# A conditioned block of linear attention and a spatial gate on one core: its projections as 64-row pairs over two token tiles

## The chip, the cores and the metric

The kernel runs on 1 core of one Trainium2 chip. The metric is device microseconds of one execution, the median of the runs shown, lower is better. TensorE is called PE below, its weight loads PEld, VectorE DVE, ScalarE ACT, GpSimd POOL and SyncE SP; SP and ACT issue the transfers.

## The reference, cut to what matters

2048 tokens of width 448 pass through two sub-blocks, each behind a normalisation whose scale and shift come from a condition vector `c`. The first sub-block is linear attention with 16 heads of 28; the second is a gated unit of half-width 896 whose gate mixes tokens with a 2048 by 2048 matrix.

```
mod = (silu(c) @ w_mod).reshape(1, 6, 1, 448)          # sa, ca, ga, sb, cb, gb
h = layernorm(x) * (1 + ca) + sa
q, k, v = split(h @ wqkv)                              # 16 heads of 28
pq, pk = q @ w_phi, k @ w_phi                          # per head
phi_q = [softmax(pq), softmax(-pq)]; phi_k likewise    # 56 features a head
kv, z = phi_k^T v, sum over tokens of phi_k
o = (phi_q kv) / (phi_q z + 1e-6)
x = x + ga * (o @ wo)
h = layernorm(x) * (1 + cb) + sb
z1, z2 = halves of gelu(h @ w_in)                      # 896 each
g = w_sp @ layernorm(z2) + b_sp
out = x + gb * ((z1 * g) @ w_out)
```

## The kernel before, in words

Tokens lie in 16 tiles of 128 (tile `i`). The width 448 is the contraction of every projection, and it lies on partitions as four blocks of 112 (`CB`, `KC` = 4), so a projection of one tile is a chain of four matmuls with 112 rows in use. A 113th row of the first block holds ones: the shift of the norm is multiplied into the weights (`SH`, `SHw`, the tile `Ga` or `Gb`), and the scale is multiplied onto the weights' rows (`SC`, `SCw`). `YB` does the shift for the half of `w_in` that is used transposed.

Everything on the main path is written as short steps, and one string, `ORDER`, lists them in the order in which they are issued: `kM:3@5` is the step `kM` for tile 3 into PSUM slot 5, a suffix `/V`, `/S`, `/G` or `/Y` picks DVE, ACT, POOL or the SP queue. Slots `A0`, `A1`, `A2` and `C` are pairs of PSUM banks, a digit is one bank. Each engine works through its own steps in the order of the string.

The steps that the text speaks of, with their lines before:

- start: `ld` loads, `l1s` statistics of a tile of `x` (L845, L846), `l1e`, `l1r`, `l1a` the normalised tile in the buffer `xpad` (L849 to L856), `X` a transpose on PE (L869) or `T1` one by a transfer (L861), both into `hT`; `ct`, `ce` the condition vector; `cs`, `cc` the columns of scale and shift (L767); `FT`, `ET`, `PF`, `EP` fold `w_phi` into the weights of k and q (L822, L828, L838).
- first stage: `kM`, `vM`, `qM` the projections (L879, L887, L927), `kE` and `kF` the two exponentials of k (L882), `qE` and `qF` those of q (L932), `vC` a copy of v, `kS`, `kR`, `kP` the softmax of k (L893, L897, L900), `kA` the sum over tokens of features times values (L910), `KV` its masked copy.
- second stage: `nM` the numerators and the two sums of a tile (L955), then on ACT `nX` and on DVE `nC`, `nS`, `nV`, `nT` (L959 to L974): a weight per head and the weighted numerators; `nA` adds the two softmax halves (L980); `T2` transposes the result, `wM` multiplies by `wo` (L990), `wR` adds it to `x` (L997), `wQ` sums its squares (L1002), `lA` to `lD`, `l2r`, `l2a` normalise again (L1010 to L1025) into `xpad`, and `T3` transposes that into `hT` over the first norm's.
- third stage: `zM` and `zG` the half that is normalised (L1036, L1040), `zQ` to `zN` its norm; `yM` and `yG` the other half (L1066, L1069), four tiles at a time.
- last stage: the gate's token product, `gM` and `pM` (L1082, L1146, the latter by seven products for eight blocks, with sums `tT` and `sS` ahead), its additions, and `oM`, `oH` the output (L1095, L1100).

Each of the last stage's matmuls uses all 128 rows. A flag, set from the largest softmax sum, chooses at the end whether a general version runs as well; it does not run here.

## Time and profile before

| what | us |
|---|---|
| median of 2 runs (248.64 to 248.87) | 248.75 |
| the profiled execution's span, first to last instruction | 246.4 |
| the profiled execution's own time | not given apart from its span |
| first k matmul | 13.67 |
| first numerators | 54.52 |
| first `zM` matmul | 74.98 |
| first matmul of the last stage on the chain | 134.15 |
| last matmul done | 241.94 |

The span leaves out what lies ahead of the first instruction and behind the last, 2.35 us between the median and the span. In the views a row names line, engine, operation, what it writes and reads, and shapes as partitions times elements. The duration of a matmul is that from its start to its modelled end; matmuls follow each other more closely than that, and the pitch is read from the chain that ended last, where a row gives the start, the time and the count of a run of matmuls.

### The profile page before, as it was taken

To read this page: it belongs to the slowest core of one execution; us is meant where nothing else is said; L and a number is where in the kernel's file an instruction comes from. 1 tells how busy PE (TensorE), PEld (TensorE's weight loads), DVE (VectorE), ACT (ScalarE), POOL (GpSimd) and SP (SyncE) were. 2 spreads that over 40 slices of the span, in tenths; PEclk is the share of its full clock that TensorE was granted. 3 is DMA by queue.
4 is the path that set the end of the run, shared out by engine and by line. 5 is a ranking of instruction groups with operands and counts; after the bars stand their busy time and mean duration, and the time that the engine had idled before them with its cause. 6 is when DMAs were issued, how large, how long until landed. Compare 5 with 4: busy or idle time off the path is not lost.

```text
span 246.4 us, 4186 instructions
## 1 busy us (share of the span) xinstructions
PE 238.6 (97%) x1505; PEld 126.3 (51%) x1513; DVE 184.2 (75%) x371; ACT 115.5 (47%) x232; POOL 125.1 (51%) x174
## 2 busy tenths in 40 slices
PE   7999999999899999999999999999999999999992
PEld 5854566665455555454444444444444544444652
DVE  3899989877998988666568983659989667386552
ACT  2899888749999797888997111000020000000000
POOL 4759986755877976965521059209239400052000
PEclk9999999999999999999999999999999999999999
DMA  7994999950226976543420870009900111000022
GB/s 188 292 284 98 213 272 201 233 141 21 64 67 150 169 133 128 129 88 85 95 33 4 170 130 0 0 3 167 197 19 3 37 56 56 3 0 3 19 71 75
DMA packets 68800, 25.23 MB, mean 102 GB/s; under 512 B 58401, under 2 KB 68642, under 8 KB 68770
## 3 DMA queue, kind: packets, MB, share of 16 engines
q1 hardware_dynamic: 68016, 24.35, 47.0%
q10 hardware_dynamic: 754, 0.52, 0.7%
q8 instruction: 14, 0.23, 0.4%
q14 instruction: 16, 0.13, 0.2%
HBM read 8.87 MB, written 1.84 MB: 43 GB/s over the span
## 4 chain that ended last, share of the span: by engine, by line
PE 92%; DVE 1%; ACT 1%; issue 1%; POOL 1%; DMA 1%; DVEq 0%; POOLq 0%
PE f_psum L1146 29%; PE f_psum L1066 10%; PE f_psum L1036 9%; PE f_psum L1095 8%; PE f_psum L927 6%; PE f_psum L1082 6%; PE f_psum L879 5%; PE f_psum L887 5%; PE f_psum L990 4%; PE f_psum L910 3%; PE f_psum L955 3%; DMA f_x<-in_A_x_dram 1%; PE f_psum L781 1%; ACT f_Eq L932 1%; PE f_psum L786 1%
## 5 line engine op out<-in xcount | busy, mean ns | idle before, releaser
L1146 PEld LDWEIGHTS <-f_z2n 128*128 128x128 bf16 x192 | 18.7, 98 | 22.4
L1146 PE MATMUL f_psum<-f_wsp,f_z2n 128*128 128x512 bf16 x119 | 27.2, 379 | 0.1
L1198 POOL TENSOR_TENSOR f_z1T<-f_gb,f_z1T 128x512 bf16<-128x512 f32 x6 | 8.4, 1411 | 35.8 <-DVE f_gb L1173 35.8
L1036 PE MATMUL f_psum<-f_win,f_hT 112*128 112x448 bf16 (+1 forms) x128 | 26.1, 352 | 0.0
L1066 PE MATMUL f_psum<-f_hT,f_win 112*128 112x512 bf16 x112 | 26.0, 379 | 0.0
L1146 PE MATMUL f_psum<-f_hT,f_Eq 128*128 128x512 bf16 x92 | 22.3, 379 | 0.2
L1166 ACT COPY f_Eq<-f_psum 128x512 f32<-128x512 f32 x4 | 2.3, 585 | 38.6 <-PE f_psum L1146 38.6
L1095 PE MATMUL f_psum<-f_wout,f_z1T 128*128 128x448 bf16 x105 | 20.4, 352 | 0.0
L1069 ACT ACTIVATE f_z1T<-f_psum,f_yb 128x512 bf16<-128x512 f32 x28 | 18.0, 682 | 1.8 <-PE f_psum L1066 1.8
L1036 PEld LDWEIGHTS <-f_hT 112*128 112x128 bf16 (+1 forms) x128 | 12.3, 97 | 11.7
L932 ACT ACTIVATE f_Eq<-f_psum 112x1024 bf16<-112x1024 f32 x16 | 15.9, 1028 | 4.3 <-PE f_psum L927 4.2
L893 DVE TENSOR_REDUCE f_ksum<-f_E 128x32 f32<-128x896 bf16 x16 | 16.8, 1064 | 1.3 <-ACT f_E L882 1.3
L882 ACT ACTIVATE f_E<-f_psum 128x448 bf16<-128x448 f32 x32 | 16.2, 565 | 2.7 <-PE f_psum L879 2.7
L974 DVE TENSOR_TENSOR f_t<-f_psum,f_w 128x896 bf16<-128x896 f32 x16 | 16.9, 1086 | 0.5
L1066 PEld LDWEIGHTS <-f_win 112*128 112x128 bf16 x112 | 10.8, 98 | 12.3
L1040 ACT ACTIVATE f_z2g<-f_psum 128x896 bf16<-128x896 f32 x16 | 14.6, 914 | 4.8 <-PE f_psum L1036 4.0
L900 POOL TENSOR_TENSOR f_phik<-f_E,f_kr 128x896 bf16<-128x896 bf16 x8 | 14.1, 1765 | 4.4 <-DVE f_kr L897 3.6
L1111 DVE TENSOR_TENSOR f_xpad<-f_psum,f_x 128x448 bf16<-128x448 f32 x15 | 9.2, 621 | 8.5 <-PE f_psum L1095 8.3
L1146 PEld LDWEIGHTS <-f_Eq 128*128 128x128 bf16 x96 | 9.4, 98 | 11.3
L1095 PEld LDWEIGHTS <-f_z1T 128*128 128x128 bf16 x105 | 10.2, 98 | 9.4
L927 PE MATMUL f_psum<-f_hT,f_Wq 113*128 113x512 bf16 (+1 forms) x64 | 15.0, 378 | 0.0
L887 PE MATMUL f_psum<-f_wv,f_hT 113*128 113x448 bf16 (+1 forms) x64 | 14.5, 352 | 0.0
(213 smaller groups left out, 498.1 us busy)
## 6 DMA issues: line engine op xcount, KB each, us to landing
out_dram<-f_xpad SPq DMA_DIRECT2D x15, 112.0 KB, 1.8
...
```

The lines of the kernel that those rows point to most:

```text
L882: nc.scalar.activation(out=Er[i % NR][:, s, :], in_=ps["k" + str(i)][:, 0, 0:D], func=ACT.Exp, scale=1.0 - 2.0 * s)
L887: nc.tensor.matmul(t[:, 0, 0:D], lhsT=hT[0:KR[m], i, m, :], rhs=wv[0:KR[m], m, :], start=(m == 0), stop=(m == KC - 1))
L893: nc.vector.tensor_reduce(out=ksum[:, i], in_=Er[i % NR][:].rearrange("p s (c f h) -> p (s c) h f", c=4, h=HP), axis=AX.X, op=ALU.add)
L927: nc.tensor.matmul(t[:, u, :], lhsT=Wq[0:KR[m], m, cc * CB:cc * CB + P], rhs=hT[0:KR[m], 4 * st:4 * st + 4, m, :], start=(m == 0), stop=(m ...
L932: nc.scalar.activation(out=Eq[st // 2][0:CB, 2 * c2:2 * c2 + 2, s, (st % 2) * 512:(st % 2 + 1) * 512], in_=ps["q" + str(n)][0:CB, :, :], f ...
L974: nc.vector.tensor_tensor(out=tr[i % 2][:], in0=numv(i)[:, :, :, 0:DH], in1=wr[i // 2 % 2][:, i % 2].unsqueeze(3).to_broadcast([P, 2, H, D ...
L1036: nc.tensor.matmul(t[:, hf, 0:D], lhsT=hT[0:KR[m], i, m, :], rhs=win_s[0:KR[m], m, FH + hf * D:FH + (hf + 1) * D], start=(m == 0), stop=(m ...
L1066: nc.tensor.matmul(t[:, 0, :], lhsT=win_s[0:CB, m, fc * P:(fc + 1) * P], rhs=hT[0:CB, 4 * st:4 * st + 4, m, :], start=(m == 0), stop=(m == ...
L1069: nc.scalar.activation(out=stage_b()["z1T"][:, fc, st * 512:(st + 1) * 512], in_=ps["y%d_%d" % (st, fc)][:, 0, :], func=ACT.Gelu_apprx_tan ...
L1082: nc.tensor.matmul(g[:, 0, 0:b - a], lhsT=later["z2n"][:, s_, fc * P:(fc + 1) * P], rhs=wspT[t][:, s_, a:b], start=(s_ == 0), stop=(s_ == ...
L1095: nc.tensor.matmul(ps["o" + str(t)][:, 0, 0:D], lhsT=later["z1T"][:, fc, t * P:(t + 1) * P], rhs=wout_s[:, fc, :], start=(fc == 0), stop=( ...
L1146: nc.tensor.matmul(t[:, 0, :], lhsT=b[:, j, f * P:(f + 1) * P], rhs=a[:, j, :], start=(PSTART[k] and j == 0), stop=(j == NH - 1), skip_gro ...
```

## The change: the width in seven blocks of 64, two token tiles on the two halves of the partitions

The width is cut into 7 blocks of 64 (`NB`, `HB`). A pair `p` of token tiles stands together: block `j` of tile 2p on partitions 0 to 63, of tile 2p+1 on partitions 64 to 127 (`HALF`). The weights are loaded twice, once for each half (`load_half`). A projection of a pair is 7 times 2 matmuls of 64 rows that alternate between the halves and write to two PSUM banks (`pairs_mm`, and the same loop in `qM`, `wM`, `zM` and `yM`). `kM`, `vM`, `wM` and `zM` now take pairs (8 of each), `yM` takes four pairs at once (14 instead of 28), and `qM` has 256 columns a matmul instead of 512.

```diff
-    def kM(i, slot):
-        t = ps["k" + str(i)] = bank(slot, "k_ps")
-        for m in range(KC):
-            nc.tensor.matmul(t[:, 0, 0:D], lhsT=hT[0:KR[m], i, m, :], rhs=Wk[0:KR[m], m, :], start=(m == 0), stop=(m == KC - 1))
+    def pairs_mm(t, p, w, n):
+        for j in range(NB):
+            for h in range(2):
+                nc.tensor.matmul(t[:, h, 0:n], lhsT=hT[HALF[h], p, j, :], rhs=w[HALF[h], j, 0:n], start=(j == 0), stop=(j == NB - 1))
+    def kM(p, slot):
+        t = ps["k" + str(p)] = bank(slot, "k_ps")
+        pairs_mm(t, p, Wk, D)
```

Scale and shift leave the weights: `SH`, `SC`, `SHw`, `SCw`, `YB`, `YE` and the row of ones are gone. `cf` and `ec` make scale and shift as columns on partitions, and `md` applies them to the transposed tiles in `hT`, in place, 128 partitions by 256 columns a step, 21 such steps for the first norm and 28 for the second; for the first two pairs the copy `XE` behind the PE transpose does it in 14 steps of 128 columns.

```diff
+    def cf(u, slot):
+        t = ps["cf%d" % u] = bank(slot, "cf_ps")
+        o = (u % 2) * D
+        for j in range(NB):
+            for kk in range(KC):
+                for h in range(2):
+                    nc.tensor.matmul(t[HALF[h], 0, j:j + 1], lhsT=wm1[:, kk, o + j * HB:o + (j + 1) * HB], rhs=scol[:, kk:kk + 1],
+                                     start=(kk == 0), stop=(kk == KC - 1))
+    def modulate(eng, out_, in_, u, j):
+        sh, sc = mods[u][:, 0, j:j + 1], mods[u][:, 1, j:j + 1]
+        if eng is nc.scalar:
+            nc.scalar.activation(out=out_, in_=in_, func=ACT.Identity, scale=sc, bias=sh)
+        else:
+            eng.tensor_scalar(out=out_, in0=in_, scalar1=sc, scalar2=sh, op0=ALU.mult, op1=ALU.add)
+    def md(u, a, b, j0, j1, eng):
+        for j in range(j0, j1):
+            v = hT[:, a:b, j, :]
+            modulate(eng, v, v, u, j)
```

`PF` is written in two column halves, 64 columns of weights each, 112 matmuls for k and q instead of 32. The sums and the numerators are pairs too: `kA` adds in two banks, one for each half of the tokens' rows, and `kb`, `kc`, `km` join them; `nM` takes four heads' 56 features on each half.

```diff
-        for s in range(2):
-            for cc in range(4):
-                o0 = s * D + cc * CB
-                nc.tensor.matmul(ps["kv"][:, s, cc * 116:(cc + 1) * 116], lhsT=pr[i % NR][:, o0:o0 + P],
-                                 rhs=vr[i % NR][:, cc * HP:(cc + 1) * HP, :].rearrange("p h f -> p (h f)"),
+        for t in range(2):
+            for a in range(8):
+                for h in range(2):
+                    nc.tensor.matmul(ps["kv"][:, h, a * 58:(a + 1) * 58], lhsT=PRT[HALF[h], p % NF, t, 2 * a:2 * a + 2, :].rearrange("p a e -> p (a e)"),
+                                     rhs=VRT[HALF[h], p % NR, t, 2 * a:2 * a + 2, :].rearrange("p h f -> p (h f)"),
-                nc.tensor.matmul(t[:, s, cc * 120:(cc + 1) * 120], lhsT=E[0:CB, cc, s, o:o + P],
-                                 rhs=KVbd[0:CB, s, cc, :, :].rearrange("p h d -> p (h d)"), start=True, stop=True)
+                for h in range(2):
+                    r = slice(HB * h, HB * h + U)
+                    nc.tensor.matmul(t[:, h, (s * 4 + cc) * 60:(s * 4 + cc + 1) * 60], lhsT=E[r, cc, s, o:o + P],
+                                     rhs=KVbd[r, s, cc, :, :].rearrange("p h d -> p (h d)"), start=True, stop=True)
```

Steps that read PSUM follow in width: `kE` 16 times 896 columns instead of 32 times 448, `vC` 8 times 896, `yG` 14 times 1024 instead of 28 times 512, `kS` 8 times 1792 columns. `wR` is always on DVE. Rings are shorter: `xpad` holds 4 pairs (8 tiles, as before), features of k 2 pairs instead of 4 tiles, the half behind `zG` 4 tiles instead of 5, outputs 5 tiles instead of 8. `cA` for the first block adds a sum that `pb` has made instead of the bias.

`ORDER` is new from end to end. Its part around the numerators, before and after:

```diff
-kA:15@A0 wos:2/V ge:1 qM:3@C qE:3 KV:1 KV:0 nM:0@A1 ... nM:1@A2 ... YB@0 ... SHw:2@1 ... qM:4@C ... SHw:3@2 ... nM:3@A2 ... nM:2@A0 ... qM:5@A1 ... zM:1@A2
+kA:7@A2 cf:3@2 kb qE:6,1 kc qM:5@A0 km:0,1 km:0,0 km:1,1 km:1,0 ... nM:0@A2 nM:1@C nX:0 nM:2@A1 ... nM:3@A0 ... nM:4@C ... nM:5@A2 ... nM:6@A0 ... nM:7@A1
+... wM:0@A2 ... nM:8@C ... nM:9@A2 ... wM:1@A1 ... wM:2@A0 ... nM:10@A1 ... nM:11@A0 ... wM:3@C ... nM:12@A2 ... nM:13@A1 ... zM:0@A0@C ... wM:4@A2 wM:5@A1
```

Before, four of the eight `qM` are issued ahead of the first `nM` and four behind it, and the first `zM` comes when ten `nM` are issued; after, all eight `qM` are ahead of the first `nM`, and the first `zM` comes behind `nM:13`. The first `zM` after needs the slots `A0` and `C`, which `nT:11` and `wR:7` leave, and both pairs of `md:1,0,2`.

On DVE the work around the first numerators stood so before (`f_cr` is written by `nC`, `f_dn` by `nS`, `f_w` by `nV`, `f_t` by `nT`, `f_win` is part of the weights that `SCw` scales):

```order
L962 TENSOR_TENSOR f_cr_101<-f_psum,f_Sx 128x32 x2
L966 TENSOR_TENSOR f_dn_103<-f_cr_101 128x32
L967 RECIPROCAL f_dn_103<-f_dn_103 128x32
L795 COPY f_yb<-f_psum 128x7
L971 TENSOR_TENSOR f_w_105<-f_Sx,f_dn_103 128x64
L974 TENSOR_TENSOR f_t<-f_psum,f_w_105 128x896 x2
L801 TENSOR_SCALAR f_win<-f_psum,f_cb_80 113x448
L944 TENSOR_TENSOR f_wout<-f_wout,f_g_rep 128x448
```

And after, where the additions to `x` (`f_x`, `wR`) of the second group begin (rows of the fourth and fifth pair of tiles):

```order
L989 SCALAR_TENSOR_TENSOR f_x,f_s_86<-f_psum,f_x 128x448 x2
L967 TENSOR_TENSOR f_w_104<-f_Sx,f_dn_102 128x64
L970 TENSOR_TENSOR f_t<-f_psum,f_w_104 128x2x2x224
L976 TENSOR_TENSOR f_oo<-f_t 128x7x64
L957 TENSOR_TENSOR f_cr_99<-f_psum,f_Sx 128x32 x2
L970 TENSOR_TENSOR f_t<-f_psum,f_w_104 128x2x2x224
L989 SCALAR_TENSOR_TENSOR f_x,f_s_86<-f_psum,f_x 128x448 x2
L961 TENSOR_TENSOR f_dn_101<-f_cr_99 128x32
L962 RECIPROCAL f_dn_101<-f_dn_101 128x32
```

The steps for a pair of tiles are the same as before; the scaling of weights between them is gone, and the additions to `x` of tiles 0 to 7 stand between the numerators, ahead of the first `zM`.

On ACT, this stood before the first two `zG` (`f_z2g`) before:

```order
L1002 ACTIVATE f_junk,f_s_88<-f_x 128x448 x2
L932 ACTIVATE f_Eq<-f_psum 112x2x512 x2
L799 ACTIVATE f_win<-f_win,f_cb_80 112x896
L959 COPY f_Sx<-f_psum 128x32 x2
L738 ACT_TABLE_LOAD
L738 ACTIVATE f_warm<-f_warm 128x1
L1040 ACTIVATE f_z2g,f_zs_91<-f_psum 128x896 x2
```

And this stands there after (`f_hx` holds `hT`, `f_mod` the columns of scale and shift):

```order
L993 ACTIVATE f_junk,f_s_87<-f_x 128x448 x4
L954 COPY f_Sx<-f_psum 128x32 x2
L782 ACTIVATE f_hx<-f_hx,f_mod_81 128x2x128 x5
L954 COPY f_Sx<-f_psum 128x32
L782 ACTIVATE f_hx<-f_hx,f_mod_81 128x2x128
L954 COPY f_Sx<-f_psum 128x32
L993 ACTIVATE f_junk,f_s_87<-f_x 128x448 x2
L1044 ACTIVATE f_z2g,f_zs_90<-f_psum 128x896 x2
```

The exponentials of q and the table load have moved ahead, and six of the seven `md` steps of the first two pairs stand directly ahead of the first `zM` and its `zG` (the seventh is on POOL).

On the SP queue the loads at the start were, before (`f_wm` are the columns of the condition's matrix for shift and scale):

```order
L664 DMA f_x<-in_A_x_dram 128x448
L653 DMA f_wq_raw<-in_A_wqkv_dram 112x4x448
L665 DMA f_x<-in_A_x_dram 128x448
L657 DMA f_phi<-in_A_w_phi_dram 112x4x28
L660 DMA f_wm_120<-in_w_mod_dram 112x4x464 x2
```

And after:

```order
L669 DMA f_x<-in_A_x_dram 128x2x448
L669 DMA f_x<-in_A_x_dram 128x448
L663 DMA f_phi<-in_A_w_phi_dram 112x4x28
L669 DMA f_x<-in_A_x_dram 128x448
L669 DMA f_x<-in_A_x_dram 128x4x448
L656 DMA f_qa<-in_A_wqkv_dram 112x4x448
L669 DMA f_x<-in_A_x_dram 128x4x448
L666 DMA f_wm_118<-in_w_mod_dram 112x4x448 x2
```

Two groups of four tiles of `x` now stand ahead of the condition's columns.

582 lines of the change are left out of this document (274 added, 308 removed).

## The prediction

> **What bounds the kernel now.** I read the page first, then who waited for whom on PE, then the chain that ended last, then the stretches between the chain's landmarks.
>
> The page's span and first part, and two rows of the waits of PE (engine and line, what it waited for, us in total, times, longest):
>
> ```profile
> span 246.4 us, 4186 instructions
> PE 238.6 (97%) x1505; PEld 126.3 (51%) x1513; DVE 184.2 (75%) x371; ACT 115.5 (47%) x232; POOL 125.1 (51%) x174
> ...
> PE f_psum L955 <- DVE f_t L974: 1.1, 2, 0.7
> PE f_psum L988 <- ACT f_Eq L932: 0.4, 1, 0.4
> ```
>
> PE is busy 97% of the time and waits 1.5 us for other engines' results after its start. So the kernel is its stream of matmuls, and less matmul time is a gain as long as nothing else takes PE's place. The chain (start, us, work, count) gives the pitches and the landmarks:
>
> ```profile
> 9.94 0.38 PE f_psum L767 x16
> ...
> 13.67 1.52 PE f_psum L879 x8
> ...
> 29.00 1.74 PE f_psum L927 x8
> ...
> 36.61 0.42 PE f_psum L910 x8
> ...
> 52.76 1.74 PE f_psum L927 x8
> 54.52 1.01 PE f_psum L955 x16
> 55.53 0.68 PE f_psum L792 x28
> 56.21 0.78 PE f_psum L786 x4
> ...
> 74.98 3.04 PE f_psum L1036 x16
> ...
> 126.38 7.77 PE f_psum L1066 x36
> 134.15 0.22 PE f_psum L1082
> ...
> 241.96 0.39 DVE f_xpad L1104
> ```
>
> A matmul of 448 columns costs 1.52/8 = 0.19 us, one of 512 columns 0.217, one of 116 columns 0.052, and one of a single column with its weight load 0.38/16 = 0.024. The last stage runs from 134.15 to 241.94 without a gap worth naming, and 4.46 us lie behind the last matmul. The stretches show how near the other engines stand to PE (busy us of PE, PEld, DVE, ACT, POOL):
>
> ```profile
> 13.67:54.52 40.85, 40.83 (x337) 24.03 (x335) 37.41 (x77) 31.76 (x62) 32.18 (x37) 1.00 0.96 206
> 54.52:74.98 20.46, 19.43 (x176) 11.69 (x177) 17.80 (x45) 18.82 (x37) 14.15 (x16) 1.00 0.23 52
> 74.98:134.15 59.17, 58.77 (x329) 29.75 (x328) 43.27 (x117) 50.24 (x108) 36.76 (x70) 1.00 0.55 103
> ```
>
> Up to 75 us DVE is busy nine tenths of the time. The stretch to look at is the second: from the first numerators to the first `zM` PE is full, and DVE at 17.80 and ACT at 18.82 of 20.46 us nearly are. PE is full there because four `qM` (6.9 us), two `SHw` (1.5) and `YB` (0.7) are put between the numerators.
>
> **The change part by part: PE's work.** No row shows two matmuls at work at once. If the two halves of a pair overlap wholly, a pair costs one stream of columns; if not at all, two, since a matmul's time goes by columns and not by the rows in use:
>
> ```profile
> L879 PE MATMUL f_psum<-f_Wk,f_hT 112*128 112x448 bf16 x48 | 11.7, 351 | 0.0
> L1095 PE MATMUL f_psum<-f_wout,f_z1T 128*128 128x448 bf16 x105 | 20.4, 352 | 0.0
> ```
>
> I take one stream, which is the assumption on which the change stands, and keep the other end as a rival. Then k, v, `wM` and `zM` are 56+56+56+112 = 280 pairs at 0.19 = 53.2 us, `yM` 98 at 0.217 = 21.3, `qM` 112 of 256 columns at half of 0.217 = 12.2: 86.7 us. Before they are 320 matmuls at 0.19 and 176 at 0.217: 99.0. That is 12.3 off, and `SH`, `SHw` (20 at 0.19) and `YB` take 4.5 more away. On: `cf` has 224 single-column matmuls for 64, 160 at 0.024 = 3.8 (half of that if its column halves overlap). `kA` and `nM` have 256 matmuls each of half the columns instead of 128: between 0.024 and half of 0.052 each, so 6.1 to 6.7 us against 6.7, nil. `PF` has 112 for 32, beside loads that PE awaits at the start anyway. Sum: 13 us less matmul work. That alone would give 246.4 - 13 = 233.
>
> **Where the 13 us go.** The new order must be followed through its landmarks. First k matmul: it needs `XE`, three steps of which stand on DVE behind ten `l1s` and the small steps of the weights.
>
> ```profile
> L845 DVE BATCH_NORM_STATS2 f_st<-f_x 128x6 f32<-128x448 bf16 x16 | 9.7, 604 | 1.1 <-DMA f_x<-in_A_x_dram 1.1
> L846 DVE BATCH_NORM_AGGREGATE f_mv<-f_st 128x2 f32<-128x6 f32 x16 | 2.9, 182 | 0.5
> L828 DVE CAST f_Wk<-f_psum 112x448 bf16<-112x448 f32 x1 | 0.6, 614 | 0.0
> L759 DVE TENSOR_TENSOR f_BD<-f_phi,f_bmask 112x448 bf16<-112x448 bf16 x1 | 0.6, 612 | 0.0
> 3.44 0.64 DVE f_st L845
> ```
>
> Ten times 0.76 (busy over count, both rows) is 7.6; three evictions at 0.62 and 0.8 for the block-diagonal in two halves are 2.7, seven steps on a few columns some 1.2: 11.5 us from about 3.5, when the first `x` is there, to 15.0, then 0.8 for `XE`. So the first k matmul starts at about 15.8 instead of 13.67. Two groups of `x` also stand ahead of the condition's columns in the SP queue now, and `cf` is no earlier for that.
>
> From there to the first numerators the order holds on PE: `kM` and `vM` 21.3, `qM` 12.2, `kA` 6.2, two `gr` 1.5, two `cf` 2.7: 43.9 us. DVE, ACT and POOL get about what they had there (less for `SC`, fewer and wider exponentials, plus 21 `md` of 0.26 to 0.55 us): 32 to 38 us each, beside PE. But k, v and q now fill pairs of banks, three of which are left once the sums hold the fourth, and the third k pair waits for `md` steps behind `kP` on POOL; I put 2.5 us for that, between 0 and 6. First numerators: 15.8 + 43.9 + 2.5 = 62.2.
>
> Then the stretch that decides. All `qM` are done, `SHw` and `YB` are gone, so until the first `zM` PE has 14 `nM` at 0.39 and four `wM` at 1.33: 10.8 us. `zM:0` waits for `nT:11` and `wR:7` on DVE. One pair of tiles costs DVE, in the timeline of before (start, us, engine, line):
>
> ```profile
> 55.66 0.31 DVE L962 TENSOR_TENSOR f_cr<-f_psum,f_Sx 128x32 f32<-128x32 f32 x2 [0.91 <-ACT f_Sx L959]
> 56.01 0.19 DVE L966 TENSOR_TENSOR f_dn<-f_cr 128x32 f32<-128x32 f32 x1
> 56.24 0.35 DVE L967 RECIPROCAL f_dn<-f_dn 128x32 f32<-128x32 f32 x1
> 56.62 0.23 DVE L971 TENSOR_TENSOR f_w<-f_Sx,f_dn 128x64 f32<-128x64 f32 x1
> 56.88 2.09 DVE L974 TENSOR_TENSOR f_t<-f_psum,f_w 128x896 bf16<-128x896 f32 x2
> ...
> L997 DVE SCALAR_TENSOR_TENSOR f_x<-f_psum,f_x 128x448 bf16<-128x448 f32 x13 | 7.8, 619 | 4.8 <-PE f_psum L990 4.8
> L997 DVE DVE_READ_ACCUMULATOR f_x<-f_psum,f_x 128x1 f32 x13 | 1.1, 81 | 0.0
> ```
>
> From 55.66 to 58.97 is 3.3 us a pair of tiles. Six pairs are 19.9 us, eight `wR` at 0.68 are 5.4, an addition and a small step 0.7: 26.0, and 0.8 from the first numerators to the first `nC`: 26.8. The other way to `zM:0` goes through tiles 2 and 3, since its pair's `md` steps also take the second pair:
>
> ```profile
> L1002 ACT ACTIVATE f_junk<-f_x 128x448 bf16<-128x448 bf16 x11 | 6.3, 574 | 1.9 <-DVE f_x L997 1.5
> L1022 POOL TENSOR_TENSOR f_v<-f_v,f_mhalf 128x2 f32<-128x2 f32 x8 | 5.9, 742 | 0.6 <-DVE f_v L1019 0.3
> L1025 POOL TENSOR_SCALAR f_xpad<-f_x,f_m,f_v 128x448 bf16<-128x448 bf16 x10 | 7.4, 747 | 0.4
> f_hT<-f_xpad SPq DMA_TRANSPOSE x15, 2.7
> L799 ACT ACTIVATE f_win<-f_win,f_cb 112x896 bf16<-112x896 bf16 x4 | 4.2, 1045 | 0.0
> L799 ACT ACTIVATE f_Wk<-f_Wk,f_ca 112x448 bf16<-112x448 bf16 x1 | 0.7, 711 | 0.0
> ```
>
> `wR:3` ends 17.7 us into the stretch (four pairs 13.2, four `wR` 2.7, 1.8 for the rest); then two sums of squares on ACT 1.5, on POOL four small steps 0.9, the power 0.74, two `l2a` 1.5 and gaps 0.5, the transpose 2.7, six `md` on ACT at 0.54 (256 columns on the line through 448 and 896) 3.3: 28.8. I take 28. So PE stands idle for 28 - 10.8 = 17 us, where before it stood for 1: the 13 us and more are given back here. First `zM`: 90.2.
>
> Behind that PE has `zM` 21.3, `yM` 21.3, four `wM` 5.3, two `nM` 0.8, and the last stage, which keeps its matmuls: 241.94 - 134.15 = 107.8. Sum 156.5. Up to the last stage PE has 48.7 us there; ACT had 50.24 in its stretch from 74.98 before, and has somewhat less with `yG` in half as many, wider steps, and DVE had 43.27, part of which now lies ahead of `zM:0`. So both are near and neither is the bound: 1.5 us of waits, between 0 and 4. Last matmul: 90.2 + 156.5 + 1.5 = 248.2. Behind it 4.46, plus 0.2 because the last addition is 448 columns and not 224 (L1104's 0.39 against 0.62): span 252.9. The median lies 2.35 above the profiled span (248.75 against 246.4): 255.2, say **255**, 2.5% more than before.
>
> [...]
>
> [...]
>
> Other edits: shorter rings (outputs 5 tiles for 8, behind `zG` 4 for 5) are covered by 1.3 us of PE work a tile, and without that cover a ring costs the landing of one transfer, about 2 us. Twice as many weight loads into SBUF are four more issues on SP, early. Neither gets a term.
>
> **The rivals.**
>
> *Weight loads come to the surface.* Each pair has two weight loads for one stream. If the second is not hidden, a slot grows by 0.024: 224 slots of the k, v and q projections and 238 behind the first `zM`, 462 x 0.024 = 11 us, 266. For it speaks that `qM`'s streams are only 0.108; against it that before a load hides under every stream. [...]
>
> *The halves do not overlap.* Then the pairs cost twice: 33.5 more ahead of the numerators, 47.9 more from `zM:0` on, none between, where PE idles: 255 + 81 = 336. [...]
>
> *Not slower: the numerators' stretch is as short as before.* Before, the first `zM` starts 20.5 us after the first numerators, with ten tiles on their way. If DVE and the chain through ACT and POOL bring `zM:0` in 20.5, for instance because they run ahead while PE is idle, the sum is 255 - 7.5 = 247.5. From 26.7 us downwards it is within 2%, and under 17 it would be faster. Against it: 26 us of DVE rows stand in that stretch, and DVE works through them in order.
>
> *Faster:* the stretch costs PE's own 10.8 us: 238. The same rows speak against it.
>
> **How the numbers follow.** Forecast with its own spread (250 to 260, from the 0 to 6 us ahead of the numerators and 27 to 30 in the stretch): 0.50. Weight loads 0.15, no overlap 0.08, short stretch 0.20, faster 0.07. The range of 80% goes from 246 to 271: below it leaves out 0.07 and a quarter of the short stretch, above no overlap (0.08); 271 is the surfaced loads' 266 with the forecast's 5 above. A measurement of this kernel can tell about 2% from no change, 243.8 to 253.7. Slower by more: 0.35 of the forecast (it straddles 253.7) and 0.23 = 0.58; within: 0.15 + 0.18 = 0.33; faster: 0.09 (0.07 and a tenth of the short stretch's).
>
> **What would show it.** First k matmul near 15.8; the chain's rows of k pairs, 14 matmuls in 1.33 us (2.66 if nothing overlaps, 1.5 with surfaced loads); PE idle about 17 us between the first numerators and the first `zM`, put down to DVE's numerators, its additions to `x` or ACT's modulation, in place of 1; PE dense from `zM:0` on, with the last stage near 108 us. The prediction is wrong if that stretch is short or full, or if a k pair does not take 1.33 us.

## The result, and the profile after

The changed kernel takes 274.7 us (273.84 and 275.56) against 248.75, a ratio of 1.104 [1.096, 1.113]: 10% slower. The forecast was 255 with a range from 246 to 271. Ratios here leave disturbed runs out, so that some differ a little from the ratio of the medians beside them.

Two rows of the page of the changed kernel, busy time by engine and the granted clock of PE in 40 slices:

```profile
PE 238.8 (88%) x2443; PEld 133.9 (49%) x2443; DVE 200.3 (74%) x380; ACT 111.7 (41%) x200; POOL 130.4 (48%) x176
PEclk9967899997975597999999999999999999999999
```

PE is as long busy as before (238.6 us), with 13 us less to do by the forecast: for a good part of the first 110 us it is granted less than its full clock, which the forecast had no term for. One row of the timeline gives the start of the first k product, and the chain that ended last gives the other landmarks (start, us, work, count; "issue" is time in which the engine waited for nothing that the profile shows):

```profile
22.70 1.87 PE L861 MATMUL f_psum<-f_Wk,f_hx 64*128 64x448 bf16 x14
```

```profile
8.46 2.01 PE f_psum L815 x40
...
13.40 0.58 PE f_psum L815 x16
...
15.36 0.57 PE f_psum L769 x30
15.92 2.70 issue
18.62 0.85 PE f_psum L769 x26
19.48 0.80 PE f_psum L815 x16
...
26.05 6.10 PE f_psum L861 x42
...
51.72 3.97 PE f_psum L861 x42
...
59.50 0.45 PE f_psum L895 x32
...
61.28 0.16 PE f_psum L895 x11
61.44 3.29 issue
64.72 0.69 PE f_psum L895 x21
...
75.22 0.87 PE f_psum L950 x47
...
86.13 2.81 PE f_psum L985 x14
...
91.62 2.81 PE f_psum L985 x14
...
105.09 1.87 PE f_psum L1039 x7
...
265.92 1.34 PE f_psum L1086 x7
```

The stretches between them, with a part of the start ahead of them (busy us of PE, PEld, DVE, ACT, POOL, then granted clock, DMA share, GB/s):

```profile
18.62:22.70 4.08, 4.08 (x73) 3.60 (x73) 1.48 (x5) 0.77 (x2) 0.84 (x2) 0.50 1.29 152
```

```profile
0.00:26.05 26.05, 19.87 (x309) 15.25 (x310) 14.97 (x46) 11.19 (x21) 13.31 (x34) 0.87 1.06 221
26.05:75.22 49.17, 43.87 (x811) 29.68 (x812) 38.63 (x55) 38.00 (x50) 31.83 (x28) 0.93 1.04 180
75.22:105.09 29.87, 15.58 (x284) 9.22 (x285) 25.38 (x63) 11.43 (x35) 18.10 (x30) 0.71 0.53 99
105.09:162.90 57.81, 55.13 (x522) 29.76 (x523) 42.87 (x111) 46.88 (x92) 40.86 (x65) 0.97 0.35 56
```

| piece | forecast, us | measured, us | late by |
|---|---|---|---|
| to the first k matmul | 15.8 | 22.7 | 6.9 |
| from there to the first numerators | 46.4 | 52.5 | 6.1 |
| from there to the first `zM` | 28.0 | 29.9 | 1.9 |
| from there to the last matmul | 158.0 | 162.2 | 4.2 |
| behind it | 4.66 | 4.64 | 0 |
| span | 252.9 | 271.9 | 19.0 |

The landmarks of the table are those of the chain. In the timeline the first numerators start at 74.88 and the first `zM` at 103.82 us, and the kernels of the experiments are compared with these two.

Two sizes were right and matter for what follows. A pair takes one stream: 42 matmuls, 21 pairs, in 3.97 us, 0.189 each. And the stretch behind the first numerators is DVE's, 25.38 of 29.87 us, with PE idle for 14.

Who made PE wait, in the first row in that stretch, in the others between the first k product and the first numerators; below them, DVE's wait for the second step of the condition's columns:

```profile
PE f_psum L950 <- DVE f_t L970: 5.7, 6, 2.4
PE f_psum L895 <- issue: 3.6, 2, 3.3
PE f_psum L861 <- DVE f_st L825: 1.5, 1, 1.5
PE f_psum L861 <- DVE f_hx L784: 1.4, 1, 1.4
```

```profile
19.51 0.17 DVE L775 TENSOR_SCALAR f_mod<-f_psum 128x7 f32<-128x7 f32 x1 [3.23 <-PE f_psum L769]
```

The largest waits ahead of the numerators, 2.70 us inside `cf:1` and 3.29 inside `kA`, stand in the middle of a run of equal matmuls and name no engine.

### The profile page after: what moved, and what is told of

Same layout as the page of the kernel before. It is cut to its first block, busy times and chain, and to the rows that moved or that the text cites. A ratio compares the mean times of both kernels' runs of the same rounds, so it can differ in the third digit from the quotient of the medians.

```text
span 271.9 us, 6032 instructions
## 1 busy us (share of the span) xinstructions
PE 238.8 (88%) x2443; PEld 133.9 (49%) x2443; DVE 200.3 (74%) x380; ACT 111.7 (41%) x200; POOL 130.4 (48%) x176
## 3 DMA queue, kind: packets, MB, share of 16 engines
HBM read 11.22 MB, written 1.84 MB: 48 GB/s over the span
## 4 chain that ended last, share of the span: by engine, by line
PE 64%; DVE 15%; DMA 7%; issue 5%; ACT 4%; POOL 4%; DVEq 0%; ACTq 0%; POOLq 0%
PE f_psum L1136 25%; PE f_psum L861 8%; PE f_psum L1086 7%; PE f_psum L1073 5%; DMA f_hx<-f_hx 5%; DVE f_t L970 4%; PE f_psum L919 3%; PE f_psum L1056 3%; PE f_psum L985 2%; ACT f_hx L782 2%; DMA f_ka<-in_A_wqkv_dram 2%; PE f_psum L1039 2%; DVE f_x L989 2%; PE f_psum L769 1%; PE f_psum L797 1%
## 5 line engine op out<-in xcount | busy, mean ns | idle before, releaser
L1136 PEld LDWEIGHTS <-f_z2n 128*128 128x128 bf16 x192 | 18.5, 98 | 22.7 <-issue 1.0
L1188 POOL TENSOR_TENSOR f_z1T<-f_win,f_z1T 128x512 bf16<-128x512 f32 x6 | 6.9, 1156 | 46.4 <-DVE f_win L1163 46.4
L1039 PE MATMUL f_psum<-f_win,f_hx 64*128 64x448 bf16 x224 | 25.3, 367 | 3.3 <-DVE f_v L1008 1.4
L1056 PE MATMUL f_psum<-f_hx,f_win 64*128 64x512 bf16 x196 | 22.7, 376 | 0.8 <-ACT f_Eq L1156 0.8
L1136 PE MATMUL f_psum<-f_hx,f_Eq 128*128 128x512 bf16 x96 | 21.7, 379 | 0.0
L1163 DVE TENSOR_TENSOR f_win<-f_psum,f_win 128x512 f32<-128x512 f32 x22 | 15.0, 688 | 7.9 <-PE f_psum L1136 7.4
L1039 PEld LDWEIGHTS <-f_hx 64*128 64x128 bf16 x224 | 12.5, 98 | 15.4 <-issue 5.0
L861 PEld LDWEIGHTS <-f_hx 64*128 64x128 bf16 x224 | 12.0, 102 | 14.2 <-issue 3.4
L985 PE MATMUL f_psum<-f_win,f_oo 64*128 64x448 bf16 x112 | 14.5, 410 | 3.9 <-DVE f_t L970 2.7
L925 ACT ACTIVATE f_Eq<-f_psum 128x1024 bf16<-128x1024 f32 x16 | 16.2, 1042 | 3.2 <-PE f_psum L919 3.2
L878 DVE TENSOR_REDUCE f_ksum<-f_E 128x64 f32<-128x1792 bf16 x8 | 16.1, 2009 | 1.4 <-ACT f_E L868 1.4
L861 PE MATMUL f_psum<-f_Wk,f_hx 64*128 64x448 bf16 x112 | 13.9, 378 | 2.8 <-DVE f_st L825 1.5
L1060 ACT ACTIVATE f_z1T<-f_psum 128x1024 bf16<-128x1024 f32 x14 | 13.9, 1020 | 2.8 <-PE f_psum L1056 2.8
```

Of the source, the lines that this page charges most:

```text
L861: nc.tensor.matmul(t[:, h, 0:n], lhsT=hT[HALF[h], p, j, :], rhs=w[HALF[h], j, 0:n], start=(j == 0), stop=(j == NB - 1))
L878: nc.vector.tensor_reduce(out=ksum[:, 2 * p + t0:2 * p + t1], in_=Er[:, p % NR, t0:t1].rearrange("p t a s (f h) -> p (t a s) h f", h=2), a ...
L925: nc.scalar.activation(out=Eq[st // 2][:, 2 * c2:2 * c2 + 2, s, o:o + 512].rearrange("p u (h q) -> p h u q", h=2), in_=ps["q" + str(n)].re ...
L985: nc.tensor.matmul(t[:, h, 0:D], lhsT=oT[HALF[h], p % NO, j, :], rhs=wo_s[HALF[h], j, :], start=(j == 0), stop=(j == NB - 1))
L1039: nc.tensor.matmul(ps["z" + str(2 * p + h)][:, hf, 0:D], lhsT=hT[HALF[h], p, j, :], rhs=win[1][HALF[h], j, hf * D:(hf + 1) * D], start=(j ...
L1056: nc.tensor.matmul(t[:, h, :], lhsT=win[0][HALF[h], j, fc * P:(fc + 1) * P], rhs=hT[HALF[h], 4 * g:4 * g + 4, j, :], start=(j == 0), stop= ...
```

## The experiments

The theories: **A**, PE's instructions arrive in blocks by a transfer, and PE stands still when a block is late in the traffic; **B**, the clock falls wherever PE idles, and costs more than the idle time; **C**, the start is late because loads and steps stand ahead of the condition's columns; **D**, the join ahead of the numerators waits behind other work. The rival to all is the forecast's own picture: engines in order, with the front set by DVE's and PE's work.

### What the stops are: e1, e17

For A speaks a count. The busy rows give the matmuls and loads that PE and PEld had started when it stopped, in the changed kernel at 15.9, 55.8 (a stop of 0.32 us) and 61.4:

```profile
0.00:15.95 15.95, 13.92 (x223) 11.12 (x224) 10.05 (x31) 7.50 (x11) 7.80 (x25) 1.00 0.97 225
0.00:61.50 61.50, 53.58 (x862) 37.37 (x863) 45.43 (x87) 42.40 (x62) 39.21 (x59) 0.92 1.06 197
0.00:55.80 55.80, 48.21 (x734) 33.38 (x735) 40.66 (x83) 37.64 (x56) 34.46 (x56) 0.91 1.05 195
```

447, 1469 and 1725: the last two are 256 apart, the first two 1022, which is four times 256 less 2 (the records need not be whole: the page of the kernel before has 1505 matmuls to 1513 loads). The test puts 42 instructions more ahead of the first stop, without more streaming:

```
-            nc.tensor.matmul(wps[:, 0, 0:256], lhsT=zero[:, 0:P], rhs=zero[:, 0:256], start=True, stop=True)
+            for _ in range(2):
+                nc.tensor.matmul(wps[:, 0, 0:128], lhsT=zero[:, 0:P], rhs=zero[:, 0:128], start=True, stop=True)
```

> The dummy matmuls of the start are issued as twice as many of half the columns: the same streaming time, 21 more matmuls with their loads (42 instructions) ahead of the second step of the condition's columns, cf:1. Theory A (PE's instructions arrive in blocks of 256, and PE stands still when the next block is late): the stop of 2.70 us inside cf:1 keeps its place in the count of PE's instructions, so it moves from behind the 30th matmul of that step to behind about the 9th, and the stop inside kA (3.29 us, behind its 11th matmul) moves out of kA into the k matmuls ahead of it. Rival (PE waits there for data, wca's second part or kP's products, and the profile doesn't name it): both stops stay where they are, at the 30th and the 11th.

The timeline of this run, and its count up to the stop:

```profile
15.29 0.32 PE L770 MATMUL f_psum<-f_scol,f_wm 112*64 112x1 bf16 x9
16.26 1.39 PE L770 MATMUL f_psum<-f_scol,f_wm 112*64 112x1 bf16 x47 [0.65 <-issue]
```

```profile
0.00:15.65 15.65, 13.61 (x223) 12.22 (x224) 9.86 (x31) 7.50 (x11) 7.58 (x25) 1.00 0.95 230
```

The stop stands behind the 9th matmul, as A had it, and at 447 again: it belongs to the count, not to the data. It is shorter too, 0.65 us. The other stops move into other steps, 1.78 us at 1469 and 1.27 at 1725 in k products and 2.20 at 2237 in a query product, and all four are 5.9 us against 6.3. The single time was 272.19.

The later experiments bear the count out. In the first 115 us, unnamed stops of 0.3 us or more stand at 447 in nine traces of the changed kernel and its other forms, at 1469 in seven, at 1725 in eight and at 2237 in seven, whatever step PE is in; the rest stand at 1213, 1981 and 2496, but for two, in e11 and e14, at 2304 and 2302, which don't fit. The traces of the old kernel and its forms have none. Timed:

> The first run's kernel, timed: 42 more instructions of PE at the start and no other change. Theory A (where the stop falls counts, since a block asked for earlier comes earlier): 1.5 to 3 us less than the changed kernel's 274.7. Rival (the stops only move, and the single time of 272.19 was its spread): 273.7 to 275.6.

270.77 us, 1.088 [1.081, 1.095]: with 42 instructions more that do nothing the time is 3.9 us less, just outside the changed kernel's own interval, which rests on two times. The single times go from 269.61 to 274.04. In its trace the stops are 4.1 us in all, and the first k product starts at 20.86, in e1's at 20.87, instead of 22.70. That shorter stops are the reason fits these rows, but e1 gains 1.5 us of span (270.4 against 271.9) with stops that are hardly shorter in sum.

The transfers during the stop in `kA` (61.4 to 64.8 us; queue, packets, MB, share of 16 engines), and the instruction queue over the whole run:

```profile
q1 hardware_dynamic: 1828, 0.52, 149.5%
q8 instruction: 1, 0.02, 2.0%
```

```profile
q8 instruction: 21, 0.34, 0.6%
...
HBM read 11.22 MB, written 1.84 MB: 48 GB/s over the span
```

The same two rows of the kernel before:

```profile
q8 instruction: 14, 0.23, 0.4%
...
HBM read 8.87 MB, written 1.84 MB: 43 GB/s over the span
```

The one packet of the instruction queue during the stop in `kA` begins between 62.25 and 62.50, the only one from 55 to 64.8; PE had stopped at 61.44 and went on at 64.72. For the first stop a packet begins between 15.75 and 16.00, as PE stops. In the kernel before, one begins between 28.5 and 29.0, as its count reaches 447, and PE does not stop.

A packet has 0.34 MB / 21 = 16 KB. PE's matmuls and loads went from 3018 to 4886, the packets of this queue from 14 to 21: 1868 / 7 = 267 instructions a packet. In the kernel before, packets begin at 109.0, 134.0, 161.5, 187.0, 214.0 and 236.5 us (each within 0.5 us), at counts from 1709 to 2951, 248 apart on average. That agrees with the steps of 256 between the stops, so I take a packet for a block of PE's instructions; the profile names the queue and not what a packet holds. Before, 256 of the 3018 last PE 246.4 x 256 / 3018 = 21 us on average, and no such stop is seen. In the changed kernel's front 256 were used up between the stops at 55.8 and 61.4, at a DMA share of 1.15.

### Fewer instructions, emptier queues: e2, e3, e5, e13, e18

e2 lets one matmul of 128 columns serve both halves of the condition's rows, the upper half one column further (`n` is 128 for six of eight columns, else 64):

```
-                for h in range(2):
-                    nc.tensor.matmul(t[HALF[h], 0, j:j + 1], lhsT=wm1[:, kk, o + j * HB:o + (j + 1) * HB], rhs=scol[:, kk:kk + 1],
+                nc.tensor.matmul(t[r, 0, j:j + 1], lhsT=wm1[:, kk, o + a * HB:o + a * HB + n], rhs=scol[:, kk:kk + 1],
```

> Each cf takes 32 single-column matmuls instead of 56: both halves of 128 rows come out of one matmul, the upper half one column further, and the small step behind it is two of half the rows. Theory A: the 449th instruction of PE now comes 96 instructions later in the work, behind cf:1, and the block arrives while PE still has others: little or no stop in cf:1, the first k matmul at 19 to 20.5 us instead of 22.7, and 2 to 4 us off the time (271 to 273). Rival (data, or the clock alone): only the 48 matmuls fewer at 17.5 ns count, 0.8 us, and a stop of about 2.7 us stays ahead of the second modulation column.

1.092 [1.083, 1.101], 271.5 by the ratio; single times from 269.6 to 275.2. The size is as A expected, the interval overlaps that of the changed kernel, so it settles nothing by itself. In its trace, of one of the longer executions, the stop at 447 is gone, but the first k product starts at 22.80 and not at 19 to 20.5: PE waits 2.5 us for the query weights instead.

The next four move loads in the SP queue (`ORDER`, short):

```
e3:  W:0,2 W:0,7 W:0,0 W:0,6 ld:bsp             -> behind T3:7,8
e5:  ld:wz0 ld:wz1 ld:wy0 ld:wy1                -> behind T2:1, T2:2, T2:3, T3:1,2 (four W:1 a little later)
e13: ld:wo0 ld:wo1 ld:wz1 ld:wz0 ld:wy0         -> behind T1:7,8 (W:0,3 later)
e18: the edit of e1, and ld:wz1                 -> behind T1:7,8
```

> Four transposing loads of the spatial weights (W:0,2, W:0,7, W:0,0, W:0,6) and the load of the spatial bias are issued behind the last transpose T3:7,8 instead of beside kA; the last stage alone reads them. Theory A, second part (the block of instructions is late because its transfer stands behind such traffic: 6 to 9 us from the start of the block before, against about 2.5 where the queues are quiet): the 3.29 us stop in kA falls under 1 us, the two k products behind it take 2.65 instead of 3.70 us as the clock stays up, and 3 to 4.5 us go off the time (270 to 272). Rival (a block takes its time whatever else moves): the stop stays at about 3 us and the time within 1 us.

279.47 us, 1.127 [1.122, 1.132]: the expectation failed. The first numerators come 3.3 us sooner (71.58), but the stop in `kA` is still there, in the chain of this run (the 6 to 9 us of the expectation run, in the changed kernel, from the start of a block in the count to the end of the stop behind it: 191 at 12.1 us to 18.62, 1469 at 55.6 to 64.72; the 2.5 are an estimate: at DMA shares of 0.60, 0.02 and 0.04 a packet has begun and ended there 1.7 to 2.5 us after the counts 1981, 2237 and 2493, at 71.2, 74.4 and 84.0 us):

```profile
59.07 2.47 issue
```

The loads of the weights, issued at 41 to 55 us, kept the queues full there without these transposing loads (DMA share 1.15 from 56 to 59 us), and the last stage's first product came at 147.1 instead of 141.6 us: PE waits 7.2 us for such a load there.

> The four loads of the gMLP's input weights (3.1 MB, each weight twice, once for each half of the rows) are issued between the transposes of the numerators' stretch instead of at 29 to 47 us; four transposing loads of the spatial weights (W:1,2, W:1,3, W:1,4, W:1,6) that stood there follow a little later. Theory A with its cause (the change loads these weights twice, the DMA engines are full to 66 us, and blocks of PE's instructions and transposes of x wait in that traffic): from 30 to 62 us the DMA share falls from above 1.0 to about 0.7, the stops at PE's 1473rd and 1729th instruction (0.3 and 3.3 us) go, the clock stays up behind them (1.0), modulations and transposes come up to 1 us earlier: first numerators 4 to 6 us sooner than 75.2, and 268 to 272 if the stretch behind them keeps its 29.9 us. Rival (the blocks are late for another reason, or the loads only move their harm): the stops stay, or the stretch grows by as much through later transposes, and the time stays within 1.5 us of 274.7.

280.35 us, 1.127 [1.121, 1.132]. The rival: the harm moved behind the numerators, where the transposes `T2` and `T3` then stand among these loads; in the traces of e5 and of e7, which has the same edit, the stretch from the first numerators to the first `zM` takes 32.2 and 33.3 us instead of 28.9.

> The changed kernel with the loads of wo, wz and one of wy (2.75 MB) issued behind the last transpose of x instead of between them, and the transposing load W:0,3 later. Theory A, narrowed: transposes of x land earlier, the modulation and the k products behind them too, fewer PE stops; first numerators at 70 to 73 instead of 75.2, 270 to 273. Rival (the bytes then run beside kA and hold PE's blocks of instructions there): the stop in kA of 3.3 us stays or grows, and the time stays within 1.5 us of 274.7.

282.39 us, 1.139 [1.135, 1.143]. A new wait took the old one's place: POOL scales `wo` ahead of its share of `kP`, and waited for it.

```profile
POOL f_win L935 <- DMA f_win<-in_A_wo_dram: 7.0, 1, 7.0
```

> The kernel of the seventeenth run (270.77) with one second load alone, the upper half of wz (0.78 MB), issued behind the last transpose of x instead of ahead of four of them; nothing needs it before the first zM. Theory A, narrowed, as in the kernel before (second loads cost 6.6 us ahead of transposes and 0.1 behind them): the four transposes land sooner, the waits for modulated tiles shrink, and the time is 267 to 269.5. Rival (in the changed kernel the front waits for so many things that one transfer less ahead of them moves nothing): 270 to 272.

273.1 us, 1.101 [1.094, 1.107]: past the rival's 272, nothing gained over e17. None of the four moves of loads helped; in e3, e5 and e13 the traces show who waits instead.

### What the second loads cost: e9, e12, e15, e16, e8

The change loads the weights of the pairs twice: 8.87 against 11.22 MB read. The kernel before can be given that alone. e9 puts a second load behind each doubled one, into SBUF that is free then:

```
 ld:wv/Y  + ld:dv/Y      ld:wo/Y + ld:do/Y      ld:win1/Y + ld:d1/Y      ld:win0/Y + ld:d0/Y
```

> The kernel before the change, with the second loads alone: wv, wo and the first half of B_w_in once more into memory that is free then, and as many bytes of the spatial weights for the other half, each behind the load that the change doubles (2.35 MB more; nobody reads them). Theory A with its cause: its first 54.5 us have a DMA share of 0.96, so the bytes lengthen them: transposes of x go from 2.7 to 4 us or more, PE waits for them, and the time grows by 3 to 8 us (251.5 to 256.5). Rival (bytes alone cost little; they need the change's many small PE instructions to hurt): within 1 us of 248.3.

258.43 us, 1.042 [1.039, 1.045]: 10.1 us more, beyond the expectation. PE waited 5.8 us for a transpose of `x`; the 12 matmuls behind it took 4.45 us instead of 2.3, and the granted clock from 35 to 60 us was 0.86 (7 us at half clock, if all of it is that, a part of them inside the wait). But later loads had to wait for the same SBUF, SP 6.3 us ahead of that of `wout`, so this is not traffic alone. e12 has them behind the last transpose `T1:14,16`:

> As the ninth run, the kernel before with the second loads alone (2.35 MB), but they are issued behind the last transpose of x (T1:14,16), not ahead of three of them, and the last one goes to the memory of the third. Theory A, narrowed (the bytes hurt because transposes of x are issued behind them and land late, PE waits 5.8 us, and runs at half clock for 6.8 us after it): without transposes behind them no wait of PE over 1 us, the clock at 1.00, first numerators at 54.5 to 56.5, 248.3 to 250.5. Rival (the front has no room for the bytes wherever they stand: weights that VectorE and GpSimd scale come later): 253 to 258.

262.09 us, 1.059 [1.052, 1.066], spoilt: its last second load overwrote a part of the spatial weights that had landed, and SP waited for the one before the other in the same memory, until `wout` came so late that PE waited 11.2 us. e15 and e16 repeat both with scratch memory in HBM as the target, for which nobody waits (this adds 2.4 MB of writes to HBM, which the change does not have):

> The ninth run again (the kernel before with the second loads of wv, wo and both halves of B_w_in, 2.35 MB, each behind the load that the change doubles), with scratch memory in HBM as their target, so that nothing waits for them. If the 10 us came from traffic: PE again waits several us for a transpose of x, the clock falls behind it, and the time is 253 to 260. If they came from what had to wait for the same SBUF memory: within 1.5 us of 248.3.

255.2 us, 1.025 [1.021, 1.030]: 6.6 us from traffic alone, the added writes included. The wait, and the timeline behind it, where four matmuls of 448 columns take 0.92 once the clock is back (last row):

```profile
PE f_psum L888 <- DMA f_hT<-f_xpad: 4.3, 1, 4.3
```

```profile
38.58 1.58 PE L888 MATMUL f_psum<-f_Wk,f_hT 113*128 113x448 bf16 x4 [4.30 <-DMA f_hT<-f_xpad]
39.96 2.75 PE L896 MATMUL f_psum<-f_wv,f_hT 113*128 113x448 bf16 x8
42.55 0.54 PE L776 MATMUL f_psum<-f_scol,f_wm 112*128 112x1 bf16 x16
42.95 0.92 PE L888 MATMUL f_psum<-f_Wk,f_hT 113*128 113x448 bf16 x4
```

4.3 us of wait, and 12 matmuls from 38.58 to 42.55 instead of 12 x 0.19 = 2.3 us, so 1.7 more, 0.57 of the full pace. The granted clock from 35 to 60 us is 0.93, and 7% of 25 us are again 1.7: theory B with its price, in a kernel whose code is otherwise the old one.

> The same second loads into scratch memory, behind the last transpose of x (the last of them behind the spatial bias). Theory A, narrowed (only what is issued behind the bytes is late): PE waits under 1 us for transposes, and what then stands behind the bytes is wout, which VectorE and GpSimd scale ahead of the numerators: 248.5 to 252. Rival (the bytes cost their own time wherever they stand): 255 to 260.

248.7 us, 1.000 [0.998, 1.002]. Its stretch from 35 us on, where these bytes now move, with PE full at full clock:

```profile
35.00:60.00 25.00, 24.89 (x268) 1.00 1.10 241
```

The same bytes cost nothing behind the last transpose. What counts between these two runs is who stands behind them in the queue. e8 takes the other way, the changed kernel without the second loads of `wo`, `wy` and `wz`; their upper halves hold zeros, so half of those products' terms are left out:

```
-ld:wo1/Y  -ld:wy1/Y  -ld:wz1/Y
+        nc.vector.memset(wbig[HB:P, 0:8192].bitcast(F32), 0.0)
+        nc.gpsimd.memset(wbig[HB:P, 8192:2 * W1 + NB * D].bitcast(F32), 0.0)
```

> The change keeps every weight of the pairs twice, once for each half of the rows, and loads it twice. This kernel leaves out the second load of wo, wy and wz (1.96 MB); the upper halves are zeros, set once at the start on VectorE and GpSimd, and half of those products' terms is left out; all instructions of PE stay. Theory A with its cause (the front is full of transfers, and PE's blocks of instructions and the transposes of x are late in that traffic): the DMA share from 28 to 66 us falls under 0.9, the stops in kA go (0.3 and 3.3 us), the first numerators come at 68 to 71 instead of 75.2, and the time is 267 to 271. Rival (the bytes are hidden, and the stops come from the count of instructions alone): the stops stay, and the time stays within 1.5 us of 274.7.

271.41 us, 1.091 [1.084, 1.098]: 3.3 us less, just past the weak end of what was expected, and its interval overlaps that of the changed kernel. In the trace the first numerators come at 72.63, 2.3 us sooner, with stops left at 447, 1469 and 2237 (0.95, 1.21 and 2.20 us). The clock of the front differs:

```profile
26.00:50.00 24.00, 22.01 (x370) 14.55 (x368) 21.04 (x37) 23.09 (x35) 18.37 (x21) 1.00 0.68 134
50.00:66.00 16.00, 14.68 (x291) 10.06 (x287) 13.86 (x14) 14.01 (x17) 11.96 (x9) 1.00 1.10 184
66.00:75.00 9.00, 5.37 (x212) 4.75 (x207) 7.08 (x18) 4.54 (x8) 2.66 (x2) 1.00 0.53 123
75.00:105.00 30.00, 15.32 (x238) 8.61 (x239) 23.32 (x56) 9.65 (x31) 18.95 (x31) 0.68 0.61 105
```

1.00 up to the numerators (0.93 before the loads were left out), and 0.68 behind them, where PE idles as much as ever. Whether that is the gain stays open: over the whole span this execution had a mean granted clock of 0.954, the other three of this kernel 0.911 to 0.936, and their times are 269.6 to 273.2 us against 272.57 here.

### The start and the join: e6, e7, e11, e14, e10

e6 loads the condition's columns first, computes them ahead of the query weights' fold, and issues six statistics later:

```
-... du:6@1 ld:x3/Y ld:wq/Y ld:x5/Y du:5@1 l1s:3 ld:wsa/Y l1s:2 ld:wca/Y ... FTq:1@3 ... FTq:0@4 ... cf:0@0 ... cf:1@1 ... X:0@6 X:1@7 ... kM:0@A0
+... ld:wsa/Y ld:wca/Y ld:wq/Y du:6@1 du:8@1 ld:x3/Y ... cf:0@2 ... cf:1@3 ... X:0@6 X:1@7 ... FTq:1@4 FTq:0@5 ... kM:0@A0
```

> The start in another order: the condition's columns wsa and wca are loaded ahead of wq and of tiles 4 to 15 of x, the gate weights and a transposing load later; VectorE makes the condition's columns ahead of the evictions of the query weights and of six statistics of later tiles; PE takes cf:0 and cf:1 ahead of the query weights' fold, and three dummies more stand ahead of the first transposes. Nothing behind the second k product is moved by more than the gate loads. Theory C (the late start, 22.7 us against my 15.8, comes from loads and steps that stand ahead of the condition's columns): first k matmul at 15 to 18 us, first numerators at 69 to 72, and 269 to 272. Rival (PE's block of instructions and its clock set the start): a stop of 2 to 4 us moves into the transposes or the first k product, which starts no earlier than 20, and the time stays within 2 us of 274.7.

283.01 us, 1.139 [1.136, 1.142]: worse, with the first numerators at 84.11. Half of C held, the transposes `X` started at 13.04 instead of 20.20 us; then the rival, with a stop in the middle of them, behind 447 matmuls and loads (223 and 224) as in the other kernels:

```profile
13.04 1.57 PE L850 MATMUL f_psum<-f_ident,f_hx 128*128 128x128 bf16 x13 [0.22 <-POOL f_hx L835]
17.84 0.26 PE L850 MATMUL f_psum<-f_ident,f_hx 128*128 128x128 bf16 x1 [3.23 <-issue]
```

> The two before together, and cf with 32 matmuls instead of 56. If theories A and C hold and their gains lie in different stages, they add: first k matmul at 15 to 17.5, first numerators at 64 to 68, no stop of PE over 1 us ahead of them, and 263 to 268. If what binds up to the numerators is the loads' bytes as a whole (they must land anyway) or VectorE's work, the gains do not add: 269 to 272.

283.07 us, 1.140 [1.136, 1.143]. Here the first k product and the first numerators start at

```profile
16.57 1.30 PE L863 MATMUL f_psum<-f_Wk,f_hx 64*128 64x448 bf16 x6
...
74.76 1.46 PE L952 MATMUL f_psum<-f_KVbd,f_Eq 56*128 56x60 bf16 x48
```

so k comes 6.1 us earlier than in the changed kernel, close to my 15.8, and the numerators 0.1. No unnamed stop of 0.3 us or more is left in the first 115 us. C falls as an explanation of the time, and so do the stops alone: both are real, and when both are gone, modulated tiles (2.3 us), the query weights (2.1), the condition's columns (1.9) and VectorE's softmax of k (1.6) make PE wait ahead of the numerators, and these come no sooner.

> The new start order of the sixth run with 32 matmuls for each cf, and without the second loads of wo, wy and wz (their products' other half is zeros). Theories A and C: what held the numerators back when the start was early was the traffic, so now both come through: first k matmul at 15.5 to 17.5, no stop of over 1 us of PE ahead of the numerators, these at 62 to 67 (my prediction had 62.2), and 260 to 266. Rival (VectorE's order in the front binds, 27.5 of the last 29.8 us ahead of the numerators in the seventh run): numerators at 70 to 75, and 269 to 276.

276.77 us, 1.111 [1.103, 1.119]: no better than the rival, with the traffic down as well. In the trace, of the longest execution, k starts at 16.50 and the numerators at 80.23.

> The run before, and without the second loads of wo, wy, wz (their half of the products is zeros), and with 32 matmuls for each cf: what is left of the change is its PE work, its order and the traffic of the kernel before. If traffic and stops of PE's instructions are what held the front, the first k matmul comes at 18 to 21, the first numerators at 64 to 68, and the time is 261 to 266, near the 255 that I had with k at 15.8 and without a term for the clock. Rival (VectorE, ScalarE and GpSimd hold the front by their order): numerators at 70 to 73, 268 to 272.

274.66 us, 1.104 [1.099, 1.110]: outside both. In its trace, of the longest execution, no unnamed stop stands ahead of the numerators, and they come at 78.26: GpSimd waits 6.2 us for `wo`, as in e13, and what e8 had gained is gone.

e10 moves `qM:6` and its exponentials behind the third numerator product:

> One query product, qM:6, with its two exponentials stands behind the third numerator product instead of ahead of the last k-v product; the gelu table is loaded behind them. Theory D (the join ahead of the first numerators, 4.1 us of one engine after the other, stands behind PE's and ScalarE's work in order): first numerators 1.5 to 2.5 us earlier, the stretch behind them at most 0.5 us longer since PE idles 14 us there, and 272 to 273.5. Rival (the stretch is bound by slots of PSUM too): it grows by 2 to 3 us, and the time stays or rises to 276.

276.19 us, 1.112 [1.108, 1.116]. The numerators come 1.9 us earlier (73.02), as D has it, and the stretch behind them grows by 3.9, to 32.8 us, more than the rival's 2 to 3. The first `wM` on the chain starts at 88.48 instead of 86.13. D brings nothing; that the query product takes a pair of PSUM banks from the numerators fits the order, but was not tried apart.

### Filling the idle time: e4

```
+    def dk(n, slot):                     # n dummies of 32 columns into columns that nobody reads
+            nc.tensor.matmul(wps[:, 0, 480:512], lhsT=zero[:, 0:P], rhs=zero[:, 0:32], start=True, stop=True)
 ... nM:2@A1 dk:40@A1 ... nM:5@A2 dk:70@A2 ... nM:7@A1 dk:60@A1 ...
```

> 306 dummy matmuls of 32 columns stand in PE's idle time between the first numerators and the first zM; nobody reads them. Theory B (the granted clock falls to half because PE idles, and the output projection, which lies on the chain twice, then takes 2.81 instead of 1.33 us): the granted clock of this stretch goes from 0.71 to over 0.95, the two wM to about 1.4, the first seven zM matmuls from 1.87 to about 0.95, and the stretch from 29.9 to 26 to 27.5 us: 270.5 to 272. Rival (VectorE's numerators set this stretch, and PE's pace is hidden): within 1 us of 274.7. Second rival: the dummies' 612 instructions bring PE stops of their own, and the time grows.

276.65 us, 1.111 [1.108, 1.115]. The stretch, and the first `wM` in it:

```profile
72.56:104.76 32.20, 23.10 (x586) 17.62 (x586) 26.38 (x64) 10.62 (x32) 17.35 (x28) 0.73 0.52 82
```

```profile
87.66 2.81 PE f_psum L989 x14
```

PE was busy for 23.1 us instead of 15.6, and its granted clock rose from 0.71 to 0.73. The attempt didn't lift the clock, so it doesn't price it; of the two `wM` on the chain only the second ran faster (1.53 us). Wider dummies were not tried. No form of the changed kernel that computes all of it beats the kernel before; the best is e17.

## Why the prediction was wrong

**The direction was right, and the reason given for it was only the smaller part.** The exchange that I described took place: matmul work falls, PE idles behind the numerators for what it gained. That stretch was forecast as 28 us and took 29.9. What failed lies mostly ahead of it.

**The step that failed** is the sum up to the first numerators, 15.8 + 43.9 + 2.5 = 62.2 us; they came at 75.2, and that is 13.0 of the 19.0 us. Three of its parts were wrong:

- *The start.* I took DVE as its limit: "three steps of which stand on DVE behind ten `l1s`", 11.5 us from 3.5. The first `x` was there at 5.5, nine of the ten were done at 16.3, and then DVE waited 3.23 us for PE. The chain runs through PE. `PF`, which I put "beside loads that PE awaits at the start anyway", stands on it with 2.01 + 0.58 + 0.80 = 3.4 us, where its two rows before were 0.41 and 0.46; `cf:1` has the stop of 2.70; and from 18.62 to 22.70 PE works at a granted clock of 0.50, which costs 2.0 of these 4.08 us. That is about the 6.9 by which k was late. The groups of `x` ahead of the condition's columns, which I named too, are no cause that the trace shows: PE has no wait for these columns.
- *PE's 43.9 us, dense and at full clock.* Between the first k product and the numerators it stood still for 3.6 us without a named reason and waited 2.9 for DVE, where I had 2.5 in all, and the granted clock was 0.93 from 26.05 on.
- *"Twice as many weight loads into SBUF are four more issues on SP, early. Neither gets a term."* I priced the issues and not the bytes, though the stretch in question had a DMA share of 0.96 in a row that I quoted. e15 and e16 give the price in the kernel before: 6.6 us ahead of transposes of `x`, nothing behind the last of them. In the changed kernel it is smaller: 3.3 us for 1.96 of the 2.35 MB (e8), with overlapping intervals.

**Two terms were missing.** No row of before shows a stop by the instruction count, nor PE at less than full clock, and I asked neither what 1870 more PE instructions need nor what an idle PE does to its clock. Behind the wait of 4.3 us in e15, 12 matmuls took 3.97 us instead of 2.3. In the start of the changed kernel the granted clock is 1.00 up to 16.0 us, 0.72 from 16.0 to 16.5 and 0.50 from there to 22.7, so it fell some 0.3 us into the stop, behind a run of single-column matmuls. How long PE must idle for that is not shown. Worked out from the rows of the changed kernel, an accounting and not a proof, since waits overlap:

- Stops by the count: 2.70 + 0.32 + 3.29 = 6.3 us. They lie on the chain; that as much time would go with them is not shown, since e7 has none and its numerators come no sooner.
- Clock: 2.0 us in the start. `wM` twice on the chain in 2.81 for 14 matmuls, where seven pairs at 0.19 are 1.33, 3.0 us; the granted clock is 0.50 in both. In the front the granted 0.93 of 49.17 us is at most 3.4 (42 matmuls take 6.10 at 26.05 and 3.97 at 51.72), and behind the first `zM` 0.97 of 57.81 is at most 1.7 (seven matmuls take 1.87 there, at 0.50). Together up to 10.1.

So up to 16.4 of the 19 us are found at their places, besides `PF`; in the front and in the numerators' stretch that is 2 us more than was missing, and behind the first `zM` 2.5 us are not found. How much of the stops and of the rest is traffic, and how much the order of the other engines, stays open: e7 and e14, which have no such stop ahead of the numerators and change other things too, gain nothing, and e7 shows a second limit of the front close behind the first.

**Point by point.** Pairs: right, 0.189 us; both rivals about them fell (surfaced loads, no overlap). `kA` and `nM`: cheaper than my bound, 0.45 / 32 = 14 ns for a matmul of `kA` against 24 to 26, some 2.6 us over its 256. First k matmul: wrong by 6.9; besides, the two rows of the statistics give 0.79 us a tile and not my 0.76, 0.3 us for the ten. The 2.5 us of waits up to the numerators: mis-sized, 6.5 us by the rows of waits. The numerators' stretch: right in its limit, and in its time partly by luck, since the 3.0 us that a granted clock of 0.50 costs on the chain were not in it. From `zM` on: PE dense as forecast, its waits of 1.5 us mis-sized by about 1, and the clock at its start missing. The tail: right.
